# The last weight rows in transfers of shrinking height, and the last two layouts made together

## The chip, the cores and the metric

The kernel runs on one core of a Trainium2 chip. The metric is device time in microseconds (us) of one execution, as the median of several runs. The profile is of one execution more, taken by the hardware profiler; its times are counted from the first instruction.

## The reference

There are two attention blocks, A and B, with the same shapes and their own data. Each decodes one token against a cache of 8192 positions with 32 heads of 128 values, in bf16. B is written as grouped attention, but has as many key heads as query heads, so nothing is shared.

```
q      = (x @ wq)                       # x 1x512, wq 512x4096 -> 32 heads of 128
scores = q . k_cache * 128**-0.5        # per head: 1x128 by 8192x128
p      = softmax(scores)
o      = p @ v_cache                    # per head: 1x8192 by 8192x128
y      = o.reshape(1, 4096) @ wo        # wo 4096x512
out    = concatenate([yA, yB])          # 1x1024
```

Per block 64 MB of keys, 64 MB of values, 4 MB of wq and 4 MB of wo are read once; nearly nothing is written.

## The kernel before, in words

**Tiling.** Heads are taken four at a time, a quad: 16 quads in all, 8 of A and 8 of B. Each of the four heads has 32 of the 128 partitions, and a partition holds 256 positions. A quad's keys are one transfer of 8 MB into one of two buffers (`kn`), its values one of 8 MB into one buffer (`vn`).

**Per quad.** VectorE multiplies the keys by q in four chunks (L333). TensorE sums over the 128 values with an identity as weights (L342). VectorE finishes the sum (L353) and takes the maximum (L359). ScalarE exponentiates (L390). TensorE multiplies the values by the probabilities, 256 small matmuls (L411), and VectorE scales the result into `oD` (L421).

**Queues.** All large transfers are issued on SyncE (SP, the line L244) in the order in which the plan is written, and they are cut over 16 DMA engines. `_Plan` holds one list of instructions for each engine, written out by hand in program order; `wait` puts a wait into an engine's list, and everything behind it in that list waits as well. Each transfer counts 16 on a semaphore when it has landed, and who needs the data waits for the count.

**The output product.** `wo` of A is one transfer. `wo` of B is cut by heads into seven groups, `WOG[1]`: heads 0-7, 8-11, 12-15, 16-23, 24-27, 28-29 and 30-31, of 128 KB for a head. Group numbers below are 0 to 6 in that order. Both go into a key buffer that has become free, and all are issued by `load_wo` (L286 to L290). The rows of a group lie as 128 partitions, so the last group, 256 KB, is 128 rows of 2 KB, one for each partition.

The product needs `o` in the layout of these rows. `plan_relayout` (L440) makes it for one group in three steps: VectorE multiplies `oD` by a mask into one of two buffers `zb` (L446), TensorE multiplies that by a selection matrix into the PSUM tile `misc` (L450), and VectorE copies `misc` to `o2` (L452). The next relayout's matmul writes `misc` too and has to wait for that copy. `plan_wo` (L455) then runs four small matmuls for each head of the group (L463), all of which add into `qyp`, once the group's `wo` and its `o2` are there.

**The end.** The last quad's values come in three pieces (`VLAST`), and behind them on SP are groups 2 to 6. TensorE multiplies the last values, `plan_o` scales them, and then TensorE's list runs:

```
        for g in early[BEFORE:]:
            plan_wo(1, g)                     # groups 2, 3, 4
        for g in range(len(early), NB):
            plan_relayout(1, g)               # groups 5, 6: they need the last quad
        for g in range(len(early), NB):
            plan_wo(1, g)                     # groups 5, 6
        plan_y(1)                             # L470: qyp to yT on VectorE
        plan_out()                            # L474, L477: turn yT, copy, store on SP
```

The relayouts of A and of groups 0 to 4 are made earlier, while the last values are still on their way.

Of the kernel before, what the change touches and what calls it, by code (L numbers as in the profile page):

```python
# [6 lines left out]
ALU = mybir.AluOpType  # L7
# [4 lines left out]
P = 128  # L12
# [11 lines left out]
class _Plan:  # L24
# [6 lines left out]
    def wait(self, eng, mark):  # L31
        if mark is None:
            return
        ctr, val = mark
        if val <= 0 or self.waited.get((eng, ctr.name), 0) >= val:
            return
        self.waited[(eng, ctr.name)] = val
        self.prog[eng].append((None, ctr, val))

    def op(self, eng, fn, ctr=None, needs=(), inc=1):  # L40

        for m in needs:
            self.wait(eng, m)
        self.prog[eng].append((fn, ctr, inc))
        if ctr is None:
            return None
        ctr.n += inc
        return ctr, ctr.n
# [81 lines left out]
def bass_concat_heads__mha_block_cached__gqa_block_cached__decode_kernel(  # L130
# [18 lines left out]
    NA = 2  # L149
# [7 lines left out]
    G = 4  # L157
# [3 lines left out]
    QA = H // G  # L161
    NM = NA * QA
    NK = 2
    CT = 64
    NCH = T // CT
# [2 lines left out]

    WOG = [[(0, 32)], [(0, 8), (8, 4), (12, 4), (16, 8), (24, 4), (28, 2), (30, 2)]]
    BEFORE = 2  # L170
    RG = [32, 16, 8, 4, 2]
    VLAST = (0, T // 2, T // 2 + CT, T)

    with ExitStack() as st:
# [3 lines left out]
        def sb(name, shape, dt):  # L178
            return ec(nc.sbuf_tensor(name, shape, dt))
# [4 lines left out]
        def flat(ap):  # L184
            return ap.rearrange("p t d -> p (t d)")
# [6 lines left out]
        wo_sb = [flat(kn[:, KW])[:, a * W:(a + 1) * W].rearrange("p (j n) -> p j n", n=NOUT)  # L192
                 for a in range(NA)]
# [15 lines left out]
        oD = sb("oD", [P, NA, H], BF16)  # L209
        zb = sb("zb", [P, 2, P], BF16)  # L210
        o2 = sb("o2", [P, NA, H], BF16)
        mask = {g: sb("mask%d" % g, [P, P // g], BF16) for g in RG}
        jsel = {g: sb("jsel%d" % g, [P, g], BF16) for g in RG}
        NQ = NOUT // P
# [3 lines left out]
        def ps(name, shape):  # L218
            return ec(nc.psum_tensor(name, shape, F32))
# [3 lines left out]
        mtp = ps("mtp", [P, 512])  # L223
        bmp = ps("bmp", [P, 512])
        misc = ps("misc", [P, 512])
# [3 lines left out]
        op, wait = pl.op, pl.wait  # L229

        def ctr(name):
            return _Ctr(nc, st, name)
# [3 lines left out]
        s_wo = [[ctr("s_wo%d%d" % (a, i)) for i in range(len(WOG[a]))] for a in range(NA)]  # L236
# [3 lines left out]
        c_pool, c_dve, c_act, c_pe = ctr("c_pool"), ctr("c_dve"), ctr("c_act"), ctr("c_pe")  # L240
        c_mul, c_red, c_sr, c_pv = ctr("c_mul"), ctr("c_red"), ctr("c_sr"), ctr("c_pv")

        def dma(eng, dst, src, c, needs=()):
            return op(eng, lambda e: e.dma_start(dst, src), c, needs, inc=16)  # L244
# [21 lines left out]
        k_in, v_in, wq_in, wo_in = {}, {}, {}, {}  # L266
        red_done, pv_done, q_done, wo_done = {}, {}, {}, {}
# [18 lines left out]
        def load_wo(a, g):  # L286
            h0, n = WOG[a][g]
            src = wos[a][h0 * Dh:(h0 + n) * Dh, :].rearrange("(p j) n -> p (j n)", p=P)
            wo_in[a, g] = dma("SP", wo_sb[a][:, h0:h0 + n, :].rearrange("p j n -> p (j n)"), src,
                              s_wo[a][g], [red_done[NM - 2, NCH - 1]])  # L290


        for a in range(NA):
# [6 lines left out]
            m = op("PE", xmm, c_pe, [x_in, i_onesb])  # L300
            x_ready = op("ACT", lambda e, a=a: e.copy(
                xb[:, a].rearrange("p c m -> p (c m)"), (misc if a == 0 else qyp)[:]), c_act, [m])
        misc_free, qy_free = [x_ready], [x_ready]
# [25 lines left out]
        mul_done, sr_done, p_done, m_done, r_done, o_done = {}, {}, {}, {}, {}, {}  # L329
# [32 lines left out]
        gm_done = {}  # L362
# [56 lines left out]
        def plan_o(n):  # L419
            a, i = divmod(n, QA)  # L420
            o_done[n] = op("DVE", lambda e: e.tensor_tensor(  # L421
                oD[:, a, G * i:G * (i + 1)], acc[:, 0:G], rinv[:, n, :], ALU.mult),
                c_dve, [pv_done[n], r_done[n]])


        sel_ready = {}

        def plan_sel():
            for g in RG:
                v = ident[:].rearrange("p (s j) -> p s j", j=g)  # L430
                op("DVE", lambda e, g=g, v=v: e.tensor_reduce(mask[g][:], v, AX.X, ALU.max),
                   c_dve, [i_ident])
                sel_ready[g] = op("DVE", lambda e, g=g, v=v: e.tensor_reduce(
                    jsel[g][:], v.rearrange("p s j -> p j s"), AX.X, ALU.max), c_dve)

        z_n = [0]
        z_free = {}
        o2_ready = {}

        def plan_relayout(a, g):  # L440
            h0, n = WOG[a][g]
            z = z_n[0] % 2
            z_n[0] += 1
            s = P // n
            zv = zb[:, z, :].rearrange("p (h s) -> p h s", s=s)
            m = op("DVE", lambda e: e.tensor_tensor(  # L446
                zv, oD[:, a, h0:h0 + n].unsqueeze(2).broadcast_to([P, n, s]),
                mask[n][:, None, :].broadcast_to([P, n, s]), ALU.mult),
                c_dve, [sel_ready[n], o_done[a * QA + (h0 + n) // G - 1 if (h0 + n) % G == 0 else a * QA + (h0 + n) // G], z_free.get(z)])
            z_free[z] = op("PE", lambda e: e.matmul(misc[:, 0:n], zb[:, z, :], jsel[n][:],  # L450
                                                    start=True, stop=True), c_pe, [m, misc_free[0]])
            o2_ready[a, g] = misc_free[0] = op("DVE", lambda e: e.tensor_copy(  # L452
                o2[:, a, h0:h0 + n], misc[:, 0:n]), c_dve, [z_free[z]])

        def plan_wo(a, g):  # L455

            h0, n = WOG[a][g]

            def mm(e):
                r = None  # L460
                for j in range(h0, h0 + n):
                    for i in range(NQ):
                        r = e.matmul(qyp[:, i:i + 1], wo_sb[a][:, j, i * P:(i + 1) * P],  # L463
                                     o2[:, a, j:j + 1], start=(j == 0 and i == 0),
                                     stop=(j == H - 1 and i == NQ - 1), skip_group_check=True)
                return r
            wo_done[a] = op("PE", mm, c_pe, [o2_ready[a, g], wo_in[a, g], qy_free[0]])

        def plan_y(a):
            qy_free[0] = op("DVE", lambda e: e.tensor_copy(yT[:, a, :], qyp[:, 0:NQ]), c_dve,  # L470
                            [wo_done[a]])
# [19 lines left out]
        for n in range(NM):  # L491
            if n >= L0:
                cuts[n].append(len(pl.prog["PE"]))
            if n + 1 < NM:
                load_k(n + 1)
            else:
                load_wo(0, 0)
                for g in range(BEFORE):
                    load_wo(1, g)
# [27 lines left out]
        NB = len(WOG[1])  # L527
        early = [g for g, (h0, n) in enumerate(WOG[1]) if h0 + n <= H - G]
        for g in range(BEFORE, NB):
            load_wo(1, g)  # L530
        plan_relayout(0, 0)
        for g in range(BEFORE):
            plan_relayout(1, g)
        plan_wo(0, 0)
        plan_y(0)
        for g in range(BEFORE):
            plan_wo(1, g)
        for g in early[BEFORE:]:
            plan_relayout(1, g)
        wait("PE", misc_free[0])  # L540
        cuts[NM].append(len(pl.prog["PE"]))
        plan_sum(NM - 1)
# [1 line left out]
            plan_pv(NM - 1, t0, t1)  # L544
        cuts[NM].append(len(pl.prog["PE"]))
        plan_o(NM - 1)
        for g in early[BEFORE:]:
            plan_wo(1, g)
        for g in range(len(early), NB):
            plan_relayout(1, g)  # L550
        for g in range(len(early), NB):
            plan_wo(1, g)
        plan_y(1)
        plan_out()
# [68 lines left out]
```

## Time and profile before

| what | us |
|---|---|
| median of 3 runs (668.53 to 668.6) | 668.54 |
| the profiled execution's own time | 668.41 |
| its span, from the first instruction to the last | 666.7 |
| PE busy | 441.5 |
| DVE (VectorE) busy | 341.5 |
| ACT (ScalarE) busy | 62.4 |
| bytes moved | 285.34 MB, at 428 GB/s over the span |
| issue of groups 2 to 6 on SP | 633.08 to 635.41 |
| issue of the output's store on SP | 665.09 |

The engines are PE (TensorE's matmuls), PEld (its weight loads), DVE, ACT, POOL and SP, the queue that issues transfers. The execution's own time is 1.7 us longer than the span, for what lies around it. In the lists of groups, waits and time, each row names line, engine, operation and tiles, with the output left of the arrow. "DMA share" in a table of stretches is the busy share of the 16 DMA engines: 1.00 is all sixteen at work, 0.50 is eight. A packet is one contiguous piece that one DMA engine moves; each engine adds one packet of 4 bytes for the count on the semaphore.

### The profile page before, as it was taken

Reading aid. Unit: us, or ns where it says so; the run is one execution under the profiler, and the core shown is the slowest. Engines: PE = TensorE matmul, PEld = TensorE weight load, DVE = VectorE, ACT = ScalarE, POOL = GpSimd, SP = SyncE. Lnnn points to the kernel's source line nnn. Section 1 sums busy time; section 2 is a strip of 40 time slices with the busy share of each in tenths; the row PEclk is TensorE's granted clock in tenths of the full one; section 3 lists DMA queues with packets and bytes.
Section 4 is the critical chain, followed back from the end, with each engine's and each line's share of the span. In section 5 each row is a group of like instructions: output and inputs, shape, how many; then the busy total and the mean of one; then the engine's idle time right before and its main releaser. Section 6 shows DMA issues by size and latency. Waiting matters only on the chain.

```text
span 666.7 us, 12274 instructions
## 1 busy us (share of the span) xinstructions
PE 441.5 (66%) x5649; PEld 252.7 (38%) x5649; DVE 341.5 (51%) x221; ACT 62.4 (9%) x151; POOL 2.8 (0%) x15
## 2 busy tenths in 40 slices
PE   2065876938487594848658484866848486685866
PEld 1022352615244261614426161442616143252646
DVE  1085818356381835638083564809356481925611
ACT  1002002020201002020100202020020202002020
POOL 1000000000000000000000000000000000000000
PEclk9998777769787776978777597877758787765875
DMA  9999999999999999999999999999999999999997
GB/s 378 440 440 437 441 431 440 425 417 433 433 436 440 433 440 437 429 417 436 433 436 440 433 440 436 436 409 436 436 436 433 436 440 436 440 409 433 413 430 292
DMA packets 6365, 285.34 MB, mean 428 GB/s; under 512 B 722, under 2 KB 724, under 8 KB 1364
## 3 DMA queue, kind: packets, MB, share of 16 engines
q1 hardware_dynamic: 6352, 285.22, 99.1%
q8 instruction: 6, 0.10, 0.1%
q14 instruction: 3, 0.02, 0.0%
q10 hardware_dynamic: 4, 0.00, 0.0%
HBM read 285.21 MB, written 0.00 MB: 428 GB/s over the span
## 4 chain that ended last, share of the span: by engine, by line
DMA 62%; PE 25%; DVE 10%; issue 1%; another core or an unknown queue 0%; SPq 0%; ACT 0%
DMA kn<-in_B_k_cache_dram 21%; DMA kn<-in_A_k_cache_dram 19%; PE rps L342 15%; DMA vn<-in_A_v_cache_dram 14%; PE acc L411 10%; DVE kn L333 9%; DMA vn<-in_B_v_cache_dram 5%; DMA kn<-in_B_wo_dram 4%; DVE s_sb L353 1%; SPq L244 0%; PE qyp L315 0%; PE qyp L463 0%; PE misc L395 0%; ACT qbc L323 0%
## 5 line engine op out<-in xcount | busy, mean ns | idle before, releaser
L342 PE MATMUL rps<-kn,ident 128*128 128x512 bf16 x1024 | 294.6, 456 | 171.7 <-DVE kn L333 171.7
L333 DVE TENSOR_TENSOR kn<-kn,qbc 128x8192 bf16<-128x8192 bf16 x64 | 281.5, 4419 | 98.3 <-DMA kn<-in_A_k_cache_dram 57.9
L342 PEld LDWEIGHTS rps<-kn,ident 128*128 128x128 bf16 x1024 | 112.6, 114 | 340.7 <-issue 266.6
L411 PE MATMUL acc<-pt,vn 128*128 128x4 bf16 x4096 | 108.7, 165 | 4.2 <-issue 2.5
L411 PEld LDWEIGHTS acc<-pt,vn 128*128 128x128 bf16 x4096 | 108.4, 100 | 4.7 <-issue 2.6
L353 DVE TENSOR_REDUCE s_sb<-rps 128x64 f32<-128x512 f32 x64 | 44.0, 688 | 112.5 <-PE rps L342 112.5
L390 ACT ACTIVATE pt<-s_sb,negb 32x256 bf16<-32x256 f32 x64 | 54.8, 857 | 2.1 <-ACT negb L382 0.2
L382 ACT ACTIVATE negb<-bmp 128x1 f32<-128x1 f32 x16 | 2.7, 171 | 529.1 <-PE bmp L378 529.1
L421 DVE TENSOR_TENSOR oD<-acc,rinv 128x4 bf16<-128x4 f32 x16 | 2.6, 162 | 88.0 <-PE acc L411 88.0
L378 PE MATMUL bmp<-gm,hrow 1*128 1x1 f32 x128 | 16.9, 249 | 6.0 <-DVE gm L368 6.0
L378 PEld LDWEIGHTS bmp<-gm,hrow 1*128 1x128 f32 x128 | 15.6, 187 | 10.7 <-DVE gm L368 10.0
L365 PE MATMUL mtp<-ident_f,m 128*1 128x128 f32 x32 | 6.1, 271 | 19.8 <-DVE m L359 19.8
L390 ACT ACTIVATION_READ_ACCUMULATOR pt<-s_sb,negb 32x1 f32 x64 | 15.9, 248 | 0.0
L365 PEld LDWEIGHTS mtp<-ident_f,m 128*1 128x1 f32 x32 | 1.4, 81 | 27.7 <-DVE m L359 27.7
L463 PE MATMUL qyp<-o,kn 128*128 128x1 bf16 x256 | 8.0, 165 | 3.9 <-issue 2.6
L315 PE MATMUL qyp<-vn,xb 128*32 128x512 bf16 x64 | 6.0, 504 | 5.7 <-DMA vn<-in_A_wq_dram 4.2
L463 PEld LDWEIGHTS qyp<-o,kn 128*128 128x128 bf16 x256 | 7.4, 103 | 4.3 <-issue 3.1
L368 DVE TENSOR_REDUCE gm<-mtp 1x4 f32<-1x128 f32 x16 | 4.5, 279 | 7.5 <-PE mtp L365 7.5
L395 PEld LDWEIGHTS misc<-rsum,ones_f 128*128 128x128 f32 x32 | 6.2, 197 | 3.6 <-issue 1.4
L359 DVE TENSOR_REDUCE m<-s_sb 128x1 f32<-128x256 f32 x16 | 6.7, 420 | 0.5
L323 ACT CAST qbc<-qyp 128x512 bf16<-128x512 f32 x4 | 2.3, 586 | 43.2 <-PE qyp L315 43.2
L297 PE MATMUL misc<-ones_bf,kn 1*128 1x128 bf16 x4 | 0.6, 302 | 7.9 <-DMA kn<-in_B_x_dram 7.9
(31 smaller groups left out, 26.6 us busy)
## 6 DMA issues: line engine op xcount, KB each, us to landing
vn<-in_A_wq_dram SPq DMA_DIRECT2D x1, 4096.0 KB, 12.2
vn<-in_B_wq_dram SPq DMA_DIRECT2D x1, 4096.0 KB, 40.4
kn<-in_A_wo_dram SPq DMA_DIRECT2D x1, 4096.0 KB, 35.2
vn<-in_B_v_cache_dram SPq DMA_DIRECT2D x1, 4096.0 KB, 15.7
vn<-in_B_v_cache_dram SPq DMA_DIRECT2D x2, 2048.0 KB, 22.5
kn<-in_B_wo_dram SPq DMA_DIRECT2D x2, 1024.0 KB, 32.4
kn<-in_B_wo_dram SPq DMA_DIRECT2D x3, 512.0 KB, 28.3
kn<-in_B_wo_dram SPq DMA_DIRECT2D x2, 256.0 KB, 28.5
```

Of the source, the lines that this page charges most:

```text
L315: r = e.matmul(qyp[hh * HP:(hh + 1) * HP, :].rearrange("p (i d) -> p i d", d=Dh), xb[:, a, c, hh * HP:(hh + 1) * HP], w, start=(c == 0), s ...
L333: mul_done[n, c] = op("DVE", lambda e: e.tensor_tensor(k, k, qbc[:, n:n + 1, :].broadcast_to([P, CT, Dh]), ALU.mult), c_mul, [k_in[n], qbc ...
L342: r = e.matmul(rps[:, c % 2, :].rearrange("p (t d) -> p t d", d=DW), ident[:], kn[:, i0, c * CT:(c + 1) * CT, i * DW:(i + 1) * DW], start= ...
L353: sr_done[n, c] = op("DVE", lambda e: e.tensor_reduce(s_sb[:, c * CT:(c + 1) * CT], rps[:, c % 2, :].rearrange("p (t d) -> p t d", d=DW), ...
L359: m_done[n] = op("DVE", lambda e: e.tensor_reduce(m1[:], s_sb[:], AX.X, ALU.max), c_dve, [sr_done[n, NCH - 1]])
L365: m = op("PE", lambda e: e.matmul(mtp[0:1, 0:P], m1[:], ident_f[:], start=True, stop=True), c_pe, [m_done[n], i_identf, gm_done.get(n - 1)])
L368: gm_done[n] = op("DVE", lambda e: e.tensor_reduce(gm[:], mtp[0:1, 0:P].rearrange("o (h p) -> o h p", h=G), AX.X, ALU.max), c_dve, [m, nb_ ...
L378: r = e.matmul(bmp[:, 0:1], hrow[0:1, h, :], gm[0:1, h:h + 1], start=(h == 0), stop=(h == G - 1))
L390: p_done[n] = op("ACT", lambda e, h=h, q=q: e.activation(pt[q, :, h], s_sb[q, :], AF.Exp, bias=negb[q, n:n + 1], scale=scale, accum_out=rs ...
L395: m = op("PE", lambda e: e.matmul(misc[:, 0:G], ones_f[:], rsum[:], start=True, stop=True), c_pe, [p_done[n], misc_free[0]])
L411: r = e.matmul(acc[:, 0:G], vn[:, t, :], pt[:, t, :], start=(t == 0), stop=(t == T - 1))
L463: r = e.matmul(qyp[:, i:i + 1], wo_sb[a][:, j, i * P:(i + 1) * P], o2[:, a, j:j + 1], start=(j == 0 and i == 0), stop=(j == H - 1 and i == ...
```

## The change

Two edits. First, the transfer of group 6, until now one of 128 partitions, is cut by partitions into 15 transfers of 15, 14, 13, 12, 11, 10, 9, 9, 8, 7, 6, 5, 4, 3 and 2 partitions, one after the other on SP and all on the same semaphore; the wait is for the sum of their counts. Second, `plan_relayout` takes up to two groups and issues their mask products, then their matmuls, then their copies; the two use `misc` and `mtp` as output. The relayouts of groups 5 and 6 are made as such a pair, and stand in TensorE's list behind the product of group 2, ahead of that of groups 3 and 4. The earlier relayouts are paired in the same way.

```diff
+    LASTP = (15, 14, 13, 12, 11, 10, 9, 9, 8, 7, 6, 5, 4, 3, 2)
...
         def load_wo(a, g):
             h0, n = WOG[a][g]
             src = wos[a][h0 * Dh:(h0 + n) * Dh, :].rearrange("(p j) n -> p (j n)", p=P)
-            wo_in[a, g] = dma("SP", wo_sb[a][:, h0:h0 + n, :].rearrange("p j n -> p (j n)"), src,
-                              s_wo[a][g], [red_done[NM - 2, NCH - 1]])
+            dst = wo_sb[a][:, h0:h0 + n, :].rearrange("p j n -> p (j n)")
+            p0 = 0
+            for k in LASTP if a == NA - 1 and g == len(WOG[a]) - 1 else (P,):
+                wo_in[a, g] = dma("SP", dst[p0:p0 + k, :], src[p0:p0 + k, :],
+                                  s_wo[a][g], [red_done[NM - 2, NCH - 1]])
+                p0 += k
...
-        z_free = {}
+        z_free, z_ps, z_read = {}, [misc, mtp], [misc_free, [None]]
...
-        def plan_relayout(a, g):
+        def plan_relayout(*groups):
+            assert len(groups) <= 2
+            made = []
+            for a, g in groups:
+                h0, n = WOG[a][g]
+                z = z_n[0] % 2
+                z_n[0] += 1
+                s = P // n
+                zv = zb[:, z, :].rearrange("p (h s) -> p h s", s=s)
+                made.append((a, g, h0, n, z, op("DVE", lambda e, a=a, h0=h0, n=n, s=s, zv=zv: e.tensor_tensor(
+                    zv, oD[:, a, h0:h0 + n].unsqueeze(2).broadcast_to([P, n, s]),
+                    mask[n][:, None, :].broadcast_to([P, n, s]), ALU.mult),
+                    c_dve, [sel_ready[n], o_done[a * QA + (h0 + n - 1) // G], z_free.get(z)])))
+            for a, g, h0, n, z, m in made:
+                z_free[z] = op("PE", lambda e, n=n, z=z: e.matmul(
+                    z_ps[z][:, 0:n], zb[:, z, :], jsel[n][:], start=True, stop=True),
+                    c_pe, [m, z_read[z][0]])
+            for a, g, h0, n, z, m in made:
+                o2_ready[a, g] = z_read[z][0] = op("DVE", lambda e, a=a, h0=h0, n=n, z=z: e.tensor_copy(
+                    o2[:, a, h0:h0 + n], z_ps[z][:, 0:n]), c_dve, [z_free[z]])
...
-        plan_relayout(0, 0)
-        for g in range(BEFORE):
-            plan_relayout(1, g)
+        z_read[1][0] = gm_done[NM - 1]
+        plan_relayout((0, 0), (1, 0))
+        plan_relayout((1, 1))
...
-        for g in early[BEFORE:]:
-            plan_relayout(1, g)
+        plan_relayout(*[(1, g) for g in early[BEFORE:BEFORE + 2]])
+        plan_relayout(*[(1, g) for g in early[BEFORE + 2:]])
...
-        for g in early[BEFORE:]:
-            plan_wo(1, g)
-        for g in range(len(early), NB):
-            plan_relayout(1, g)
-        for g in range(len(early), NB):
+        plan_wo(1, BEFORE)
+        plan_relayout(*[(1, g) for g in range(len(early), NB)])
+        for g in range(BEFORE + 1, NB):
             plan_wo(1, g)
```

The three loops of the new `plan_relayout` issue the same instructions as the body of the old one.

## The prediction

> **What bounds the kernel now.** I read the chain of waits first. By line it is transfers for 62% of the span; the transfer engines are busy nearly to the last slice, so only the end can move. The chain from 655 us to the end:
>
> ```profile
> 634.03 28.26 DMA kn<-in_B_wo_dram
> 662.29 0.05 issue
> 662.34 0.59 PE qyp L463 x16
> 662.92 0.05 PE misc L450
> 662.97 0.02 issue
> 663.00 0.16 DVE o L452
> 663.16 0.21 DVE zb L446
> 663.37 0.05 issue
> 663.41 0.19 PE misc L450
> 663.60 0.21 PE qyp L463 x8
> 663.81 0.04 issue
> 663.85 0.39 PE qyp L463 x8
> 664.24 0.02 issue
> 664.26 0.17 DVE yT L470
> 664.44 0.04 issue
> 664.48 0.28 PE bmp L474
> ```
>
> The transfer that ends the chain is group 4, landed at 662.29. Behind it stand 16 matmuls and the two relayouts of groups 5 and 6, one after the other. Group 6's own matmuls start at 663.85. The landing record of its semaphore reads 661.51 for the first of the 16 engines and 663.57 for the last, so the last piece is 0.28 us early: the relayouts decide, barely.
>
> Next the table of stretches, whose column after PEclk is the share of the 16 DMA engines still at work:
>
> ```profile
> 661.50:662.00 0.50, 0.50 (x23) 0.50 (x19) 0.00 (x0) 0.00 (x0) 0.00 (x0) 0.50 0.48 184
> 662.00:662.50 0.50, 0.26 (x10) 0.17 (x8) 0.00 (x0) 0.00 (x0) 0.00 (x0) 0.50 0.43 164
> 662.50:663.00 0.50, 0.45 (x17) 0.37 (x14) 0.00 (x1) 0.00 (x0) 0.00 (x0) 0.50 0.23 86
> ```
>
> 0.48 x 16 is about eight engines: half are done by 661.5, half still carry their last rows. The landings agree: eight between 661.51 and 661.84, one at 662.13, seven from 662.79 to 663.57. Their mean is 662.41. That unevenness is what a height-graded transfer could use.
>
> **Which engines are late.** The transfer view gives the queues:
>
> ```profile
> q1 hardware_dynamic: 6352, 285.22, 99.1%
> q10 hardware_dynamic: 4, 0.00, 0.0%
> ```
>
> q10 carries the two x loads of one partition each: four packets, two rows and two counts. So a one-partition transfer runs on one engine. q1 has 16 packets more than the rows and counts of the 44 full-height transfers (44 x 16 engines x 9 = 6336): the store of 8 partitions, on 8 engines. The row that speaks to the shape of the new transfers is therefore one engine for each partition, k engines for k partitions. I take the engine of the x loads as the one that all 15 take part in. In the packet records the second x row (6.28 us) lies between two wq rows, ending 6.283 and starting 6.322, so its engine can be followed by ends and starts. That engine is the one which at 53.4 us shares its time with a 16 KB instruction packet, of 986 ns, and from there on it is late; in the last stage its final packet starts at 662.63 (first engine 661.01, last 663.11).
>
> The same holds for the other late ones. Each instruction packet of 16 KB (53, 82, 90, 97, 644, 650 us) made one engine late, by 1.2 to 1.5 us as the landing records before and after it show, each time another one; two fall in the stretch from 642 to 652.5 us:
>
> ```profile
> DMA packets 254, 4.26 MB, mean 406 GB/s; under 512 B 32, under 2 KB 32, under 8 KB 32
> ...
> q8 instruction: 2, 0.03, 1.3%
> ```
>
> **The change, part by part.**
>
> *Relayouts as a pair.* In the time list the mask product of group 5 ends at 660.12 (659.83 + 0.29). That of group 6 now follows at once, ending near 660.4; the two matmuls follow (0.17 and 0.19), then the copies (0.16 each), and all is done by about 661. They lie in the gap before TensorE's matmuls of group 3, whose data lands at 661.03. They need an idle 0.5 us of TensorE between 660.43 and 661.08; without it group 3 would shift, with 0.24 us of idle time before group 4 as second cover. So they cost nothing and leave the chain. What is late next: group 4's 16 matmuls end at 662.92, group 5 lands at 662.94, its 8 matmuls (0.39 by the last row of them) run 662.99 to 663.38, and group 6 starts at the later of 663.38 and its landing + 0.05 (the step from 662.29 to 662.34). With the landing of before, 663.57, it would start at 663.62 and gain 0.23 us. The most that both edits can gain is 663.85 - 663.38 = 0.47 us.
>
> *The 15 transfers: issue.* Fourteen more issues on SP at 0.43 us (five took 2.33) and 0.04 between end SP's block near 642 rather than 635.4. Behind them on SP is only the store at 665.09, and the data is needed at 661: covered by 19 us. Nothing else of the plan moves on SP or POOL.
>
> *The 15 transfers: rows.* Before, each engine has 8 rows of 2 KB, which start 80 ns apart. With k engines for k partitions, engine 0 and 1 get 15 rows, then 14, 13, 12, 11, 10, 9, 8, 6, 5, 4, 3, 2, 1 and 0. From one transfer's count to the next one's first row the packet records show 6 ns, for each further transfer. The x loads' engine, late already, gets 7 rows more and 14 counts more: 7 x 0.080 + 14 x 0.006 = 0.64. Its last packet moves from 662.63 to 663.27, and with 0.46 from packet to landing (663.11 to 663.57) it lands at 663.73. The other five engines that instruction packets made late ended between 0.33 us before it and 0.3 us after it. If these fetches go round the engines in order, as one engine after another being hit suggests, they are engines 1 to 5. The worst is then the third, some 0.2 us later than engine 0 and with 6 x 0.080 + 13 x 0.006 = 0.56 added: 661.01 + 1.84 + 0.56 + 0.46 = 663.87. Bounds: 663.73 if all the others are high-numbered; 664.21 (663.57 + 0.64) if the latest engine of all is engine 1. I take 663.87, the sum for the order that the fetches suggest.
>
> *The sum.* Group 6 starts at 663.87 + 0.05 = 663.92 instead of 663.85, and all behind it is unchanged: +0.07 us, between -0.07 and +0.41. Against the profiled execution 668.41 gives 668.48. That one stands 0.13 below the median 668.54, so the median should become 668.6. The first edit's 0.23 us is spent by the second.
>
> The price of one more transfer on an engine is the weakest term. The nearest row is the 6 ns between full-height transfers, but there at least 8 rows lie between two counts, and here one. The far end is a whole 0.46 us from packet to landing, if an engine finished each count before it began the next row: 14 x 0.46 = 6.4 us. Below nothing it cannot be, since the rows are the same bytes. I take 6 ns, because rows behind a count show no wait for its landing.
>
> The Trainium skill (DMA: Bandwidth & Descriptors, Rules for kernel authors) speaks against the edit: many small transfers should be merged, since under 64 KB one mostly pays overhead; the page's anatomy section puts about 2.0 us of fixed cost on a transfer on the GpSimd path. Paid one after another, 14 x 2.0 would be an estimated 28 us; no row here shows such a cost behind a queued transfer. The same page (Why a DMA increments its semaphore by 16 and not by 1) says that a transfer uses the largest number up to 16 that divides the partitions, on the lowest-numbered engines; the trace agrees on the number (1 and 8), and shows no engine's number.
>
> **The rivals.**
>
> 1. *The wedge fits.* The late engines are the high-numbered ones, and the x loads' engine is not among those that get 15 rows. Then the last lands at 663.57 - 0.64 = 662.93, and group 6 starts at its floor 663.38: -0.47 us, median 668.1. For it: the heights fall steadily. Against: the engine of the one-partition transfers is late. Still within the bound below.
> 2. *Transfers do not follow back to back* (slower). Fifteen counts on one engine, one row apart, each cost part of the landing time. It decides for "slower" once group 6 starts 1.34 us later, at 665.19: engine 0's last packet then starts at 664.68, which is 663.19 without the counts plus 14 x 0.106. At the full 0.46 it is 663.19 + 6.44 + 0.46 + 0.05 = 670.14, +6.3 us. SP gives the same sign if it can't have 22 transfers under way: before, at most 10 were issued and not landed. For: no row shows counts so close. Against: the 6 ns.
> 3. *Other engines are late* (faster). The instruction packets fall elsewhere, or not in the end at all, and all engines end together: landings move from 663.57 to 662.41, 1.16 sooner, for groups 4 to 6 alike, and with the 0.47 that is 1.6 us. For: TensorE's list changes. Against: only by where two matmuls stand.
>
> **How the numbers follow.** About 0.2%, 1.34 us, is what a measurement of this kernel can tell from no change. The forecast has 0.53, the first rival 0.20, the second 0.22, the third 0.05. Forecast and first rival are within the bound, 0.73 together. The range begins below the first rival, at 667.9, leaving out the third. Upward it takes the forecast's bounds and reaches into the second rival to a price of about 0.14 us a transfer, 670.4, where I put 0.09 of its 0.22: left out are 0.05 and 0.13.
>
> **What would show it.** Right: both copies L452 of two heads before 661.3, no L450 in the chain behind group 4, the last product released by the transfer between 663.75 and 664.3, and all 16 landings of other groups as before. The first rival: the last product starts at about 663.4 behind the matmuls of group 5. The second: the share of DMA engines stays low and above zero well past 664, with gaps between rows of 2 KB. The third: group 4 lands before 662. I am wrong altogether if the time leaves 667.2 to 669.9.

## The result, and the profile after

The change makes the kernel slower: 670.68 us against 668.54, median of 7 runs each, a ratio of 1.0033 with a 95% interval of 1.0023 to 1.0043. That is 2.1 us more, above the predicted range, which ended at 670.4, and above the 1.34 us that the prediction called the bound. The profiled execution's span is 668.8 us against 666.7.

The end of the chain of waits of the changed kernel (start, length, what):

```profile
650.99 14.89 DMA kn<-in_B_wo_dram
665.88 0.14 issue
666.02 0.37 PE qyp L475 x8
666.38 0.02 issue
666.41 0.17 DVE yT L482
```

No relayout is in it any more. The last of the 15 transfers is issued at 650.99 and has landed at 665.88; group 6's eight matmuls start at 666.02, where they started at 663.85 before. All behind them is unchanged. TensorE's list in order of time, with the idle time before each row in brackets:

```profile
659.76 0.58 PE L475 MATMUL qyp<-o,kn 128*128 128x1 bf16 x16 [0.25 <-issue]
660.20 0.17 PE L460 MATMUL misc<-jsel,zb 128*128 128x2 bf16 x1
660.30 0.19 PE L460 MATMUL mtp<-jsel,zb 128*128 128x2 bf16 x1
661.43 1.01 PE L475 MATMUL qyp<-o,kn 128*128 128x1 bf16 x32 [0.95 <-DMA kn<-in_B_wo_dram]
662.81 0.59 PE L475 MATMUL qyp<-o,kn 128*128 128x1 bf16 x16 [0.37 <-DMA kn<-in_B_wo_dram]
663.66 0.35 PE L475 MATMUL qyp<-o,kn 128*128 128x1 bf16 x8 [0.26 <-DMA kn<-in_B_wo_dram]
666.02 0.35 PE L475 MATMUL qyp<-o,kn 128*128 128x1 bf16 x8 [2.01 <-DMA kn<-in_B_wo_dram]
```

The two relayouts (L460) lie at 660.2 to 660.5, in the idle time before group 3. The idle time before groups 3 to 6 is waiting for transfers. The last landings of groups 3, 4 and 5 are at 661.38, 662.76 and 663.52, where they were at 661.03, 662.29 and 662.94 before, although nothing of their own transfers was changed. In the stretch in which the early engines move group 6 and the late ones still group 4, less is moved than before, with no fewer engines at work. The row of before (PE, PEld, DVE, ACT, POOL, then the clock, the share of DMA engines at work, GB/s):

```profile
661.00:661.50 0.50, 0.42 (x15) 0.42 (x16) 0.00 (x0) 0.00 (x0) 0.00 (x0) 0.50 0.75 283
```

The rows of the changed kernel, of which the last ones show a second loss:

```profile
661.00:661.50 0.50, 0.07 (x2) 0.07 (x3) 0.00 (x0) 0.00 (x0) 0.00 (x0) 0.50 0.83 225
...
663.50:664.00 0.50, 0.34 (x8) 0.30 (x8) 0.00 (x0) 0.00 (x0) 0.00 (x0) 0.50 0.07 25
664.00:664.50 0.50, 0.01 (x1) 0.00 (x0) 0.00 (x0) 0.00 (x0) 0.00 (x0) 0.50 0.00 0
664.50:665.00 0.50, 0.00 (x0) 0.00 (x0) 0.00 (x0) 0.00 (x0) 0.00 (x0) 0.50 0.00 0
665.00:665.50 0.50, 0.00 (x0) 0.00 (x0) 0.00 (x0) 0.00 (x0) 0.00 (x0) 0.50 0.00 0
```

After 664.06 no DMA engine moves anything, yet the last count lands at 665.88: the data has been moved, and for 1.8 us the core waits for counts. Before, the last packet, a count, was at 663.11 and its count landed 0.46 us later. The transfer view shows how many there are:

```profile
q1 hardware_dynamic: 6464, 285.22, 98.9%
```

6464 - 6352 = 112 packets more with the same bytes: 128 counts of group 6 instead of 16.

From the packet records, the latest engine has its last packet of group 5 at 662.93, instead of 662.47, and its last of all at 664.06. These 1.126 us are 13 rows and 13 counts (13 x 0.086; 8 rows and one count took 0.645). So its three losses are:

| on the engine that ends last | before | after | difference |
|---|---|---|---|
| its last packet of group 5 | 662.47 | 662.93 | +0.47 |
| its rows and counts of group 6 | 0.645 | 1.126 | +0.48 |
| from its last packet to the landing | 0.46 | 1.82 | +1.36 |
| last landing | 663.57 | 665.88 | +2.31 |

(The differences are made from unrounded times.) Of the 2.31 us, 0.28 were slack, and the start follows 0.14 us behind the landing: 666.02 - 663.85 = 2.17, which is the difference of the two spans within 0.1.

### The profile page after: what moved, and what is told of

Same layout as the page of the kernel before. It is cut to its first block, busy times and chain, and to the rows that moved or that the text cites. A ratio compares the mean times of both kernels' runs of the same rounds, so it can differ in the third digit from the quotient of the medians.

```text
span 668.8 us, 12288 instructions
## 1 busy us (share of the span) xinstructions
PE 439.3 (66%) x5649; PEld 252.7 (38%) x5649; DVE 341.1 (51%) x221; ACT 62.4 (9%) x151; POOL 2.8 (0%) x15
## 3 DMA queue, kind: packets, MB, share of 16 engines
q1 hardware_dynamic: 6464, 285.22, 98.9%
## 4 chain that ended last, share of the span: by engine, by line
DMA 65%; PE 23%; DVE 9%; SPq 3%; issue 1%; ACT 0%
DMA kn<-in_B_k_cache_dram 21%; DMA kn<-in_A_k_cache_dram 18%; DMA vn<-in_B_v_cache_dram 14%; PE rps L348 12%; PE acc L417 10%; DMA vn<-in_A_v_cache_dram 9%; DVE kn L339 8%; SPq L245 3%; DMA kn<-in_B_wo_dram 2%; DVE s_sb L359 1%; PE qyp L321 0%; ACT qbc L329 0%; PE misc L401 0%; PE qyp L475 0%; PE bmp L486 0%
## 5 line engine op out<-in xcount | busy, mean ns | idle before, releaser
L348 PE MATMUL rps<-kn,ident 128*128 128x512 bf16 x1024 | 291.6, 453 | 172.0 <-DVE kn L339 172.0
```

What stands on the lines that cost most here:

```text
L348: r = e.matmul(rps[:, c % 2, :].rearrange("p (t d) -> p t d", d=DW), ident[:], kn[:, i0, c * CT:(c + 1) * CT, i * DW:(i + 1) * DW], start= ...
```

## The experiments

The theories: (1) counts stand in a line, an engine lands one every 0.18 us, and many short transfers pile them up; (2) the heights give more rows to late engines; (3) the rows of the short transfers slow the rows that the late engines are still moving, which is called crowding below. Edits are against the changed kernel unless said otherwise. "4 KB rows" is the mean length of the packets of 4096 B that start from 661.0 to 661.5 us, which are rows of group 4 on the late engines while the early ones move group 6 (11 to 17 packets of one execution for each kernel).

| kernel | counts on an engine | last packet | last landing | from packet to landing | 4 KB rows, ns | median, us |
|---|---|---|---|---|---|---|
| before | 1 | 663.11 | 663.57 | 0.46 | 164 | 668.54 |
| changed | 13 (the latest) | 664.06 | 665.88 | 1.82 | 226 | 670.68 |
| r_only | 1 | 663.11 | 663.57 | 0.46 | 164 | 668.31 |
| w_only | 15 at most | 664.12 | 665.95 | 1.83 | 249 | 670.70 |
| e16c | 8 | 663.57 | 664.95 | 1.38 | 265 | 669.77 |
| e16s | 8 | 664.19 | 665.53 | 1.34 | 282 | 670.12 |
| w_sems | 15 at most | 663.95 | 665.82 | 1.87 | 249 | 670.79 |
| e32 | 4 | 663.72 | 664.38 | 0.66 | 254 | 669.04 |
| w4 | 4 at most | 663.74 | 664.24 | 0.50 | 247 | 669.03 |
| id8 | 2 at most | 664.56 | 665.12 | 0.56 | 276 | 669.78 (one run) |
| c4 | 4 | 663.33 | 663.84 | 0.51 | 163 | 668.46 |
| c2 | 2 | 663.14 | 663.59 | 0.45 | 164 | 668.27 |
| few12 | 13 | 664.32 | 665.59 | 1.27 | 162 | 670.09 |

The medians of the kernel before, measured beside them, were 668.42 to 668.54.

### r_only: the relayouts as a pair, group 6 in one transfer

```diff
-    LASTP = (15, 14, 13, 12, 11, 10, 9, 9, 8, 7, 6, 5, 4, 3, 2)
+    LASTP = (128,)
```

> Relayouts as a pair, group 6 again one transfer of 128 partitions. All theories: the landings are those of before (last near 663.57), the relayouts leave the chain, and group 6's matmuls start right behind the landing, about 663.62 instead of 663.85: -0.2 us, median 668.3. If the pair itself costs the 2 us, then 670 or more.

Measured: 668.31 us, ratio 0.9997 (0.9988 to 1.0006). Its chain:

```profile
635.00 28.57 DMA kn<-in_B_wo_dram
663.57 0.14 issue
663.70 0.37 PE qyp L475 x8
```

The last landings of groups 3 to 6 are those of before, to the hundredth; the matmuls start 0.15 us sooner, at 663.70. So the pair does what was forecast, only that the step from landing to matmul is 0.14 us here and not 0.05. A gain this small lies inside the interval.

### w_only: the 15 transfers, relayouts as before

The edit is the first half of the change alone, put into the kernel before.

> The 15 transfers, relayouts as before. Theory 1 (the counts of many short transfers land late) and theory 2 (more rows on late engines) agree: the last landing, 665.88 after the change, decides alone and hides the relayouts again, so 670.7 within 0.2 us. If the two parts share the loss, it is clearly below 670.4.

Measured: 670.70 us, ratio 1.0032 (1.0019 to 1.0044), last landing 665.95. The whole loss is in the transfers.

### e16c and e16s: even heights, eight transfers of 16

```diff
-    LASTP = (15, 14, 13, 12, 11, 10, 9, 9, 8, 7, 6, 5, 4, 3, 2)
+    LASTP = (16,) * 8
```

In e16s the rows of transfer i are `slice(i, 128, 8)` instead of 16 neighbours.

> Group 6 as 8 transfers of 16 neighbouring partitions: 8 rows on every engine as before, but 8 counts instead of 1. Theory 1 (counts on one engine land 0.18 us apart while rows with counts follow 0.086 apart): the last packet stays within 0.5 us of 663.11, but lands 0.46 + 7 x 0.094 = 1.1 us after its packet, near 664.8, and the median is 669.2 to 669.6. Theory 2 (uneven heights load the late engines): heights are even, landing near 663.6, median 668.4.

> The same 8 transfers, but each takes every eighth partition, so that the rows moved at one time are not neighbours. Theory 1 alone: the same time as with neighbours, within 0.2 us. Theory 3 (neighbouring rows get in each other's way, and slow the rows of 4 KB of the late engines from 159 to 226 ns): the rows of 4 KB take 159 ns again, and up to 0.5 us of the loss is gone.

Measured: 669.77 us (ratio 1.0020, 1.0011 to 1.0029) and 670.12 us (1.0021, 1.0012 to 1.0030). Both are above what theory 1 gave (669.2 to 669.6, and no more than 0.2 us between the two). With even heights more than half of the loss is still there, so theory 2 alone falls. The step from packet to landing is 1.38 and 1.34 us, as theory 1 gives within 0.3. In e16s the last four landings are one engine's, and lie 0.18 us apart (664.99, 665.17, 665.35, 665.53). The packets are longer still than with neighbours, 282 ns against 265, so that neighbouring rows crowd each other is not it either. What both have in common with the change is that their rows crowd the others somehow: theory 3 was left, without its reason.

### w_sems: a semaphore for each transfer

```diff
-                wo_in[a, g] = dma("SP", dst[p0:p0 + k, :], src[p0:p0 + k, :],
-                                  s_wo[a][g], [red_done[NM - 2, NCH - 1]])
+                wo_in.setdefault((a, g), []).append(dma(
+                    "SP", dst[p0:p0 + k, :], src[p0:p0 + k, :],
+                    s_wo[a][g] if p0 == 0 else ctr("s_wp%d" % p0), [red_done[NM - 2, NCH - 1]]))
...
-            wo_done[a] = op("PE", mm, c_pe, [o2_ready[a, g], wo_in[a, g], qy_free[0]])
+            wo_done[a] = op("PE", mm, c_pe, [o2_ready[a, g], *wo_in[a, g], qy_free[0]])
```

> The changed kernel with a semaphore of its own for each of the 15 transfers, and TensorE waiting for all 15. Theory 1a (an engine lands its counts 0.18 us apart, whatever they count on): last landing at 665.9 again, median 670.7 within 0.3 us. Theory 1b (only counts on one and the same semaphore stand in a line): the last lands about 0.46 us after its packet at 664.06, and the median falls by 1.3 us to 669.4.

Measured: 670.79 us, ratio 1.0035 (1.0022 to 1.0048), packet to landing 1.87 us. The line is the engine's and not the semaphore's: the last landings of the latest engine are 665.10, 665.28, 665.46, 665.64 and 665.82, each on another semaphore.

This run also tells the engines apart. A transfer of k partitions shows k landings, beside one record at its issue, and they fall into an early and a late bunch about 1 us apart. Transfers of 15, 14, 13, 12, 11, 10, 9, 8, 7, 6, 5, 4, 3 and 2 have 7, 7, 7, 6, 5, 4, 3, 3, 3, 2, 1, 1, 0 and 0 late ones. If a transfer of k uses engines 0 to k-1, then engines 3, 5, 6, 9, 10, 11 and 12 are late in this execution. The x loads' engine, 0, is early.

### e32 and w4: few counts, even heights and falling ones

```diff
-    LASTP = (15, 14, 13, 12, 11, 10, 9, 9, 8, 7, 6, 5, 4, 3, 2)
+    LASTP = (32,) * 4
```

In w4 it is `(45, 39, 24, 20)`.

> Group 6 as 4 transfers of 32 partitions: 8 rows on every engine, and 4 counts, one behind every second row, so 0.166 us apart. Theory 1 (0.18 us from count to count on one engine is what decides): nearly nothing piles up, 4 KB rows take 160 to 180 ns, the last landing is at most 0.3 us behind that of one transfer (663.57), median 668.3 to 668.7. A fixed price for each transfer (after e16c, about 1.45 us for 7 more of them, 0.2 each) gives 3 x 0.2 = 0.6 us: 668.9.

> Heights that fall as in the change, with few counts: 4 transfers of 45, 39, 24 and 20 partitions, so that engines 0 to 9 get 10 rows, 10 and 11 get 8, 12 gets 6, 13 and 14 get 3 and 15 none; at most 4 counts on an engine, 0.166 us or more apart. Theory 1 with late engines among the low-numbered ones: the last lands 0.1 to 0.3 us later than with one transfer (663.57 + 2 x 0.08 + little), median 668.4 to 668.8. If the late engines were the high-numbered ones, group 6 would start at its floor near 663.4, median 668.1.

Measured: 669.04 us (ratio 1.0008, 0.9999 to 1.0017) and 669.03 us (the same interval). Both expectations by theory 1 missed, by 0.34 and 0.23 us; nearer came the other price in the first one, 0.2 us for each further transfer (668.9), which c4 tests. Against the kernel before, neither loss is clear of its interval, so the reading rests on the traces. The step from packet to landing is small, 0.66 and 0.50 us, but the 4 KB rows take 250 ns though hardly any counts pile up. So piled-up counts do not cause the crowding: it is a loss of its own. Even and falling heights give the same time here.

### id8: 120 partitions and 8

```diff
-    LASTP = (15, 14, 13, 12, 11, 10, 9, 9, 8, 7, 6, 5, 4, 3, 2)
+    LASTP = (120, 8)
```

Each transfer has a semaphore of its own, as in w_sems.

> Group 6 as a transfer of 120 partitions (15 engines, 8 rows each, engine 15 none) and one of 8 (engines 0 to 7, one row each) on a semaphore of its own, whose 8 landings show how late each of the engines 0 to 7 is. If the six instruction packets fell on engines 0 to 5, six of the eight landings lie 1.2 us or more behind the first. If they fell on others, most of the eight are early. Time within 0.3 us of the run with one transfer, 668.3.

Measured, in one run: 669.78 us. Five of the eight landings of the short transfer are early (662.01 to 662.93) and three late (663.77, 664.16, 665.12), as w_sems says: three of the engines 0 to 7 are late. The expected time was missed by 1.5 us. With two transfers and hardly a count more, the 4 KB rows take 276 ns. Some of that time is this run's own: its latest engine was 2.82 us behind the first in group 2 already, against 2.14 in the profile of before. What a transfer of 120 shares with all the others that crowd, and not with one of 128, may be where its rows go: 120 over 15 engines, 32 over 16 or 16 over 16 can put each engine's rows on other partitions than 128 over 16 does. No trace shows which partitions an engine gets. It is not the number of rows: each engine has 8 here, as with 128.

### c4 and c2: the same partitions, cut by columns

```diff
-            for k in LASTP if a == NA - 1 and g == len(WOG[a]) - 1 else (P,):
+            m = dst.shape[1]
+            q = 4 if a == NA - 1 and g == len(WOG[a]) - 1 else 1
+            for i in range(q):
+                cols = slice(i * m // q, (i + 1) * m // q)
+                wo_in[a, g] = dma("SP", dst[:, cols], src[:, cols],
+                                  s_wo[a][g], [red_done[NM - 2, NCH - 1]])
```

In c2 it is `q = 2`.

> Group 6 as 4 transfers of all 128 partitions and a quarter of each row (512 B): as many transfers and counts as in e32, but every engine writes the same partitions as in one transfer. Theory 3' (rows on partitions that belong to another engine in a full-height transfer slow that engine): the 4 KB rows of the late engines take 160 to 170 ns as with one transfer, not 254, the last landing is near 663.7, median 668.3 to 668.6. If the number of transfers is what slows them: 250 ns and 669.0 as in e32.

> Group 6 as 2 transfers of all 128 partitions and half of each row: 2 counts on each engine, some 0.33 us apart, partitions as in one transfer. Theories 1 and 3' together: as with one transfer within 0.15 us, 668.3 to 668.45.

Measured: 668.46 us (ratio 1.0000, 0.9991 to 1.0009) and 668.27 us (0.9997, 0.9988 to 1.0007). The same stretch in e32 and then in c4, both with four transfers and four counts on an engine:

```profile
661.00:661.50 0.50, 0.05 (x1) 0.05 (x2) 0.00 (x0) 0.00 (x0) 0.00 (x0) 0.50 0.79 193
```

```profile
661.00:661.50 0.50, 0.33 (x12) 0.34 (x13) 0.00 (x0) 0.00 (x0) 0.00 (x0) 0.50 0.93 299
```

In pieces of all 128 partitions the engines move 299 GB/s in this half microsecond, and in pieces of 32 partitions 193; for each engine at work (0.93 and 0.79 of sixteen) that is about 20 and 15. The 4 KB rows take 163 ns again, group 3 lands at 661.12 and not at 661.41, and all eleven times of c4 (668.18 to 668.82) lie below all eleven of e32 (668.83 to 669.40). So the number of transfers is not what crowds, and theory 3 holds: it is the cut by partitions. The size of the pieces is not it either, for one transfer of 2 KB rows (r_only) does not crowd and neither do rows of 1 KB (c2). A row's partition and its place in memory change together in these cuts, so the runs do not tell which of the two it is.

### few12: twelve counts more and nothing else

```diff
+            if a == NA - 1 and g == len(WOG[a]) - 1:
+                for i in range(12):
+                    few[0] = dma("SP", scr[:, 32 * i:32 * (i + 1)], wos[a][0:16, 0:32], s_few)
```

This stands at the head of `load_wo`, in r_only, with a scratch tile `scr`; SP waits for the twelve at the very end.

> Group 6 as one transfer, and ahead of it on the queue 12 transfers of 16 rows of 64 B that nobody waits for before the end (added work: a scratch tile). Heights and partitions of group 6 are those of one transfer, so only 12 more counts on each engine are left. Theory 1 (0.18 us from count to count on an engine): its first small count lands near 662.95 on the latest engine and group 6's count 12 x 0.18 later, at 665.1, group 6's matmuls start near 665.25, median 669.6 to 670.1. If counts are free: 12 x 0.02 for the small rows, 668.5.

Measured: 670.09 us, ratio 1.0025 (1.0016 to 1.0034). Group 6 is one transfer, the 4 KB rows take 162 ns, and still 1.8 us are lost against r_only. 1.27 us pass from its last packet to its landing, with counts 0.18 us apart.

That last packet is itself 1.2 us later than in r_only, and the small rows are not the reason: on the engine that ends last, a 64 B row and its count take 13 ns together, 0.16 us for all twelve. But sixteen 2 KB rows, as many as there are engines, take 0.79 to 1.04 us each, where the longest of r_only takes 0.096. On the latest engine it is the third row of group 6 (0.96 us), and costs 0.87 us; the other 0.17 is a later start, left unexplained. The stretches show the late engines nearly standing, and going on:

```profile
662.50:663.00 0.50, 0.37 (x14) 0.37 (x15) 0.00 (x0) 0.00 (x0) 0.00 (x0) 0.50 0.20 22
663.00:663.50 0.50, 0.38 (x16) 0.33 (x13) 0.00 (x0) 0.00 (x0) 0.00 (x0) 0.50 0.24 94
```

So an engine does not move rows freely behind any number of counts. No run separates whether the long row waits for the counts or for the small rows. The expected end holds all the same, because the line of counts runs meanwhile.

The line of counts gives the end of six kernels within 0.07 us. Take the last landing of group 5 and add 0.18 us for each count behind it on the engine that ends last, taken to be the same engine: 663.52 + 13 x 0.18 = 665.86 for the change (measured 665.88), 663.50 + 8 x 0.18 = 664.94 for e16c (664.95), 664.09 + 8 x 0.18 = 665.53 for e16s (665.53), 663.64 + 4 x 0.18 = 664.36 for e32 (664.38), 663.05 + 4 x 0.18 = 663.77 for c4 (663.84) and 663.20 + 13 x 0.18 = 665.54 for few12 (665.59). Before and in c2 the rows take longer than the line, and they decide.

## Why the prediction was wrong

**The failed step is the price of one more transfer on an engine.** It was taken as 6 ns, from the start of the next row behind a count, with 0.46 us from the last packet to its landing as before; those 0.46 became 1.82. The row behind a count says when the engine goes on; it does not say when the count lands, and the semaphore waits for landings. An engine lands its counts 0.18 us apart. Before, they were issued 0.65 us apart or more, and the limit could not show. Behind single rows they are issued 0.086 us apart, so each adds up to 0.18 - 0.086 = 0.094 us; 12 more give 1.13, measured 1.36. The rest lies in group 5's count, which stands ahead of them in the line: it lands 0.59 us behind its packet instead of 0.46, and the line is one step longer.

The second rival put a cost in this place. It decides for "slower" once group 6 starts at 665.19, at 0.106 us for each of 14 transfers. Group 6 started at 666.02, and 1.36 us over the 12 more transfers of the engine that ends last are 0.113 each. The sign that it named did not come: the rows follow each other without gaps, and the engines are idle from 664.06 on. The late start of 2.17 us would have passed the bound of 1.34 without the next term too (2.17 - 0.47 = 1.70); what carried the median past the top of the range is the next term (670.68 - 0.47 = 670.21, within 670.4).

**A term was left out: the crowding, 0.47 us.** The sum held groups 3 to 5 at their landings of before. e32 against c4 shows that pieces cut by partitions slow the engines that are still behind. The Trainium skill (SBUF — State Buffer, Door 1: The DMA port swizzle) says that partitions share 16 ports in sets such as 0-3 with 32-35, that 16 neighbours reach four of them, and that in a transfer of 128 each engine serves one port. The trace agrees in kind: 299 GB/s with pieces of 128 partitions and 193 with pieces of 32. The page would have spoken against the change, and the prediction did not weigh it. That ports are the reason is not shown: no run here shows a port, and e16s, which by the page's table reaches eight ports instead of four, was no better than e16c. The reason for the crowding stays open.

**Which engines are late was wrong as well.** The x loads' engine was followed through the packet records to the instruction packet at 53.4 us, but three engines' rows start within 6 ns of each other just before it (51.031 to 51.037), and the chain could change over between them. By w_sems engine 0 is early, and the late ones are 3, 5, 6 and 9 to 12: neither the forecast's order nor the first rival's. That is another execution, with the engines numbered as said there; in id8, too, three of the engines 0 to 7 are late. The prediction also counted six late engines, one for each instruction packet of 16 KB, where seven landings are late: from the transfer that lands at 177 us on, one more engine is 1.2 us behind the first, and an instruction packet of 8 KB lies at 167 us. The price of a row was right: 13 rows on the engine that ends last, which by the heights is engine 3, cost 0.48 us, and the prediction's prices give 5 x 0.080 + 12 x 0.006 = 0.47. That its 0.56 for another engine is near is luck.

**Right were** the relayouts (they left the chain, done by 660.7, and the pair alone is not slower), SP's issue as covered, and the store and the steps behind the last product. The step from landing to product was 0.14 us instead of 0.05. SP took longer than forecast:

```profile
632.65 18.95 SPq L245 DMA_DIRECT2D kn<-in_B_wo_dram  x19
```

The issue ends at 651.6 and not at 642; single issues took up to 2.6 us. That still lies 9 us ahead of the first row of group 6.

The best of the versions are r_only and c2, 0.23 and 0.15 us below the kernel before, measured beside them; neither is clear of its interval.

## What to carry to other kernels

If a late transfer has to be cut, cut it by columns rather than by partitions, so that every piece is a full-height transfer, and keep the counts on one engine further apart than the time it needs to land one, 0.18 us here. A gap between packets prices what an engine does; what a waiting instruction sees is the landing, and the two should be measured separately before many small pieces are queued. When a tail is uneven over engines, find out which engine is which, by short transfers on semaphores of their own, before giving any of them less.

## What the runs showed of the hardware that was not expected

- An engine lands counts 0.18 us apart, on one semaphore (e16s) or on several (w_sems). With counts 0.086 us apart it goes on moving rows meanwhile; behind 13 counts 13 ns apart one row takes 0.96 us on the engine that ends last, and sixteen rows in all take 0.79 to 1.04 us (few12).
- Beside transfers of 2 to 120 partitions, the 4 KB rows of other engines take 226 to 282 ns instead of 164. Beside full-height pieces, and beside few12's rows of 64 B, they take 162 to 164.
- SP's issue waits when much is queued: the fourth of the 15 pieces took 2.6 us, and later ones mostly 0.6, 1.2 or 2.4, which are about the times of one 16 KB row (0.61), one 32 KB row (1.22) and two of these. That the wait ends when an engine has taken queued rows is a reading of these times, not tested.
